# A recurrent-memory transformer and mixer kernel: each engine's instructions in one line of ranks, in place of a greedy pick

## The chip, the cores and the metric

One NeuronCore of one Trainium2 chip. The metric is the device time of one launch in microseconds (us), the median of the runs shown; lower is better.

## The reference, cut to what matters

```
x = A_x                                  # (1, 2048, 640), bf16
x = x + A(LN(x)); x = x + B(LN(x))       # layer 1
x = x + A(LN(x)); x = x + B(LN(x))       # layer 2, the same weights

A(x): mem = mem0                         # 8 rows
  for s in range(64):                    # segments of 32 rows
    h = concat([mem, x[32*s : 32*s+32]]) # 40 rows
    q, k, v = h @ Wq, h @ Wk, h @ Wv     # 32 heads of 192
    p = softmax(mask(q @ k.T / sqrt(192)))
    o = (p @ v) @ Wo                     # 40 rows x 640
    mem = o[:8]; out[s] = o[8:]

B(x): h = gelu(LN(x) @ w1)               # 640 x 640
      hs = (quarters of h, shifted by 1 or 2 rows down or up) @ w2
      x1 = x + hs
      return x1 + gelu(LN(x1) @ w3) @ w4 # 640 x 1536, 1536 x 640
```

The eight memory rows that come out of a segment go into the next one, so the 64 segments of a layer run one after the other.

## The kernel before

**Steps.** The kernel runs 69 steps, `t` = 0 to 68. Step `t` computes attention on segment `t` of layer 1 and on segment `t` - 5 of layer 2 (`LAG = 5`), as two "lanes" side by side in the same matmuls. Steps 0 to 4 have the first lane alone, steps 64 to 68 the second alone; the 59 steps between them have both. From step 2 on, every second step also starts a "chunk" of B (64 rows of each lane): `chunk` holds the layer norms, w1, w2 and w3, `chunk_end` w4 and the stores. So the kernel has a period of two steps, called a pair below: an even step, which carries `chunk`, and an odd one.

**Work of a step.** The 32 heads are taken in eight groups of four. The names below are those of the inner functions of `attention_step`:

| function | engine, lines | what it does for a group |
|---|---|---|
| `keys_queries.fn` | TensorE (PE), L1106 | keys (`psk`) and queries (`psq`), 6 or 18 matmuls at a time |
| `fk`, `fk2`, `fq` | VectorE (DVE) L1125 and L1132, ScalarE (ACT) L1117 | copies of keys and queries to SBUF |
| `values3.fv`, `values.fv` | PE, L1162 (two lanes), L1202 (one) | values of two groups; the array is split into 32 or 64 wide columns |
| `v_copy.fe` | ACT L1142 (with one lane DVE too) | copies of the values |
| `attend.fs` | PE, L1222 | scores `pss` |
| `f1`, `f2`, `f3` | DVE L1234, ACT L1241, DVE L1245 to L1247 | mask and row minimum, exponential, normalization |
| `f4`, `f5` | PE L1257, ACT L1265 | transposes of the probabilities, copy to `PT` |
| `f6`, `f7` | PE L1274, ACT L1282 | probabilities times values, copy to `oT` |
| `project.f8` | PE, L1300 | two blocks of 15 matmuls with Wo, accumulated over all groups in `psy` |

When all 16 blocks of `f8` are in, DVE copies the memory rows (`fm`, L1327) into the next step's `hT`, whose first keys and queries wait for that. In the chunk, `transposes` (L1380) follow a layer norm (L1354 to L1356 on DVE, L1364 on GpSimd, L1370 on DVE), and the sums of w2 (L1660) enter one through L1677.

**Weights.** A part of Wq, Wk, Wv and all of Wo is kept in SBUF (`res_tile`, L963); the rest is streamed in every step through a ring of 12 buffers `wst` (`load_pair`, L979), and w1 to w4 through 3 buffers `wstB` (`load_b`, L1015). All these loads are issued by SyncE (SP), one after the other.

**The order.** The functions above are not called where they stand. `Plan.add` records each as an operation with its engine, an estimated duration, a due time, its predecessors and the PSUM or ring buffers that it needs; `Plan.place` then decides in which order all 20,033 operations are issued, and with it which of the interchangeable buffers each gets. In `place`, time goes on by estimates. An operation is a candidate once its predecessors are placed. Of an engine's candidates that could start within 0.12 us (PE) or 0.05 us (the others) of the earliest, the one with the lowest rank `op.pr` goes first; while PE is in a split-array mode, operations of that mode go ahead. The two queues of loads, `wa` and `wb`, are each in order of due time. The flag `keep` holds back one or two PSUM buffers from some operations.

The rank is a number from the table `RANK` plus the start of the step. All even steps with two lanes share one list (`step0`), the odd ones another (`step1`); the one-lane steps have `step0a`, `step1a`, `step0b`, `step1b`; steps 0, 1 and 68 have lists of their own, and the chunks four kinds.

A load can also get a wait that the data does not ask for: where the plan holds it back (`op.paced`), it waits for a PE operation placed shortly before.

Of the kernel before, what the change touches and what calls it, by code (L numbers as in the profile page):

```python
# [20 lines left out]
LAG = 5  # L21
# [26 lines left out]
LAT = 0.07  # L48
# [21 lines left out]
        "apply_ln.f": (40.666, 77.653, 60.325, 136.543,),  # L70
        "chunk.f1": (149.945,),
        "chunk.f2": (216.417,),
        "chunk.f3": (155.176,),
        "chunk.fe": (75.977,),
        "chunk.fe3": (198.054,),
        "chunk.fel": (228.91,),
        "chunk.fhr": (61.777,),
        "chunk.fhs": (218.218,),
        "chunk.fk0": (191.856,),
        "chunk.fk1": (121.846,),  # L80
        "chunk.fs": (49.786, 151.703,),
        "chunk.ft": (158.562,),
        "chunk.fw": (42.803, 169.943, 29.392, 148.529, 90.1, 11.697, 135.335, 134.874, 211.529, 268.509, 163.859,
            -14.712, 124.067,),
        "chunk.fx": (133.776,),
        "chunk.fx0": (137.067, 177.953,),
        "chunk.fxu": (58.634,),
        "gelu.f1": (101.378, 21.338, 126.119, 33.51, 52.11, 75.508, 54.74,),
        "gelu.f2": (-97.492, 94.341, 84.288, 173.304, -56.927, 147.711, 109.223,),
        "gelu.f3": (153.483, 118.045, 87.113, 42.669, 49.105, 150.693, -76.347,),  # L90
        "gelu.f4": (215.512, 20.666, 98.392, 164.337, 98.395, -19.815, 38.198,),
        "ln_ops.f1": (134.07, 148.183,),
        "ln_ops.f2": (224.099, 88.099,),
        "load_b.fn": (223.389, -19.177, -20.646, 90.639, 9.322, 217.551, 18.597, 62.818, 70.516, 168.406, 246.054,
            -38.876, 264.694,),
        "transposes.f": (51.17, -12.814, 36.007,),
    },
    "chunk_0": {
        "apply_ln.f": (94.572, 40.674, 99.984, 157.869,),
        "chunk.f1": (191.077,),  # L100
        "chunk.f2": (131.998,),
        "chunk.f3": (54.83,),
        "chunk.fe": (62.439,),
        "chunk.fe3": (144.847,),
        "chunk.fel": (188.349,),
        "chunk.fhr": (111.798,),
        "chunk.fhs": (35.35,),
        "chunk.fk0": (279.891,),
        "chunk.fk1": (172.8,),
        "chunk.fs": (-35.996, 198.001,),  # L110
        "chunk.ft": (-130.725,),
        "chunk.fw": (65.065, 183.661, 25.703, 78.053, 99.658, 101.601, 99.809, 59.563, 88.798, 111.146, 143.476,
            55.339, -78.899,),
        "chunk.fx": (54.138,),
        "chunk.fx0": (87.873, 36.59,),
        "chunk.fxu": (99.398,),
        "gelu.f1": (126.71, -29.076, 155.641, 51.835, 147.033, 124.243, 168.393,),
        "gelu.f2": (78.921, 274.88, 137.606, 151.483, 27.132, 58.196, 59.089,),
        "gelu.f3": (117.084, 46.08, 158.262, 0.249, 28.271, 95.39, 62.133,),
        "gelu.f4": (76.679, 104.557, -54.1, 110.658, 151.139, 33.853, 164.863,),  # L120
        "ln_ops.f1": (54.318, 149.368,),
        "ln_ops.f2": (235.942, 114.803,),
        "load_b.fn": (92.037, 17.038, 113.343, 48.931, -19.849, 68.172, 137.659, 98.815, 95.648, 183.418, 66.865,
            -12.07, 10.81,),
        "transposes.f": (-24.285, -1.559, -116.16,),
    },
    "chunk_1": {
        "apply_ln.f": (60.831, 149.44, 32.185, 134.603,),
        "chunk.f1": (170.297,),
        "chunk.f2": (62.735,),  # L130
        "chunk.f3": (43.465,),
        "chunk.fe": (95.975,),
        "chunk.fe3": (173.951,),
        "chunk.fel": (25.923,),
        "chunk.fhr": (176.191,),
        "chunk.fhs": (114.575,),
        "chunk.fk0": (206.574,),
        "chunk.fk1": (238.724,),
        "chunk.fs": (118.505, 102.403,),
        "chunk.ft": (99.656,),  # L140
        "chunk.fw": (-11.005, 57.564, 28.334, 134.891, 126.429, 158.993, 107.2, 142.84, 61.226, 94.852, 116.376,
            8.48, 114.245,),
        "chunk.fx": (83.335,),
        "chunk.fx0": (-20.333, 52.005,),
        "chunk.fxu": (148.101,),
        "gelu.f1": (28.271, 94.572, 36.624, 95.274, 14.56, 53.144, 63.864,),
        "gelu.f2": (37.136, 133.251, 134.956, 64.362, -76.106, 19.116, 161.678,),
        "gelu.f3": (21.295, -102.923, 161.628, 76.35, 65.44, 109.028, 174.762,),
        "gelu.f4": (174.545, 97.124, 142.652, 141.694, 60.364, 76.871, 132.958,),
        "ln_ops.f1": (162.228, 148.321,),  # L150
        "ln_ops.f2": (235.566, 107.308,),
        "load_b.fn": (145.113, 225.966, 12.701, -9.013, 112.357, 1.949, 84.958, -9.104, -18.176, 31.005, 172.224,
            55.576, 114.018,),
        "transposes.f": (96.899, 66.044, -38.11,),
    },
    "chunk_2": {
        "apply_ln.f": (8.202, 39.685, 192.795, 133.254,),
        "chunk.fe": (190.072,),
        "chunk.fe3": (84.469,),
        "chunk.fel": (198.164,),  # L160
        "chunk.fhr": (103.491,),
        "chunk.fhs": (185.145,),
        "chunk.fk0": (111.508,),
        "chunk.fk1": (163.798,),
        "chunk.fs": (161.524, 76.874,),
        "chunk.ft": (26.979,),
        "chunk.fw": (98.577, 144.019, -18.584, 159.176, 43.005, 108.193, 111.764, 32.15, -26.496, 216.749, 7.779,
            10.758, 3.409,),
        "chunk.fx": (120.989,),
        "chunk.fxu": (78.836,),  # L170
        "chunk.fz": (166.304,),
        "gelu.f1": (62.309, 171.702, 48.166, -74.106, 94.517, 171.311, 114.397,),
        "gelu.f2": (67.833, 145.055, 4.726, 204.533, 99.365, 118.038, 58.3,),
        "gelu.f3": (23.209, 88.075, 155.923, 172.275, 169.817, 76.866, 110.477,),
        "gelu.f4": (248.488, 170.71, 206.421, 32.421, 181.585, 40.743, 63.89,),
        "ln_ops.f1": (58.912, 167.818,),
        "ln_ops.f2": (190.32, 246.267,),
        "load_b.fn": (216.599, 23.043, 172.357, 161.103, 73.744, 88.447, 84.661, -8.871, 26.089, 19.475, 66.634,
            -0.164, 128.784,),
        "transposes.f": (155.883, 38.197,),  # L180
    },
    "chunk_end": {
        "apply_ln.f": (74.666,),
        "chunk_end.fc": (70.51, -35.564, 44.026,),
        "chunk_end.fs": (87.765, 84.744,),
        "chunk_end.fst": (209.154, 130.81,),
        "chunk_end.ft4": (41.154,),
        "chunk_end.fw": (135.537, 72.945, 58.938, 109.724, 176.111, -20.18,),
        "chunk_loads.f": (216.414, 82.152, 214.202, 66.482, 114.965,),
        "ln_ops.f1": (147.277,),  # L190
        "ln_ops.f2": (123.156,),
        "load_b.fn": (12.735, -55.921, -67.147, 236.411, 24.651, 132.479,),
    },
    "chunk_end_0": {
        "apply_ln.f": (55.229,),
        "chunk_end.fc": (45.352, 234.489,),
        "chunk_end.fs": (50.063, 260.419,),
        "chunk_end.fst": (132.001,),
        "chunk_end.ft4": (146.259,),
        "chunk_end.fw": (318.093, 80.971, 109.238, 226.518, 174.396, 112.588,),  # L200
        "chunk_loads.f": (173.64, 236.626, 258.971,),
        "ln_ops.f1": (164.537,),
        "ln_ops.f2": (229.895,),
        "load_b.fn": (-80.145, 213.968, -54.408, 81.572, -5.558, 174.34,),
    },
    "chunk_end_1": {
        "apply_ln.f": (202.88,),
        "chunk_end.fc": (212.408, 176.723, 92.891,),
        "chunk_end.fs": (267.017, 127.574,),
        "chunk_end.fst": (80.687,),  # L210
        "chunk_end.ft4": (92.094,),
        "chunk_end.fw": (-44.134, 54.695, -10.468, 58.676, 84.616, 115.287,),
        "chunk_loads.f": (114.578, 103.494, 47.28, 166.009, 84.391,),
        "ln_ops.f1": (114.276,),
        "ln_ops.f2": (159.369,),
        "load_b.fn": (21.697, 78.816, -48.919, 11.318, 1.33, -117.781,),
    },
    "chunk_end_2": {
        "apply_ln.f": (134.851,),
        "chunk_end.fc": (113.219, 106.317, 211.498,),  # L220
        "chunk_end.fs": (59.427, 147.204,),
        "chunk_end.fst": (183.717, 30.774,),
        "chunk_end.ft4": (172.85,),
        "chunk_end.fw": (73.12, 14.739, 137.062, -11.873, 7.708, 235.266,),
# [351 lines left out]
class Plan:  # L576
# [57 lines left out]
    def place(self):  # L634
        in_queue = {}
        head = {}
        for q, lst in self.queues.items():
            lst.sort(key=lambda o: (o.due, o.i))
            for k, o in enumerate(lst):
                in_queue[o.i] = (q, k)  # L640
# [1293 lines left out]
```

## Time and profile before

| | |
|---|---|
| median of 3 runs | 3257.11 us (3255.47 to 3259.9) |
| profiled execution: span from first to last instruction | 3252.3 us |
| profiled execution: own time | not listed apart from the span; the span lies 4.8 us under the median |
| PE matmuls / weight loads (PEld) busy | 3142.1 us (97%) / 2780.2 us (85%) |
| DVE / ACT / POOL busy | 2274.2 us (70%) / 1833.8 us (56%) / 269.7 us (8%) |
| read from HBM | 816.98 MB, 253 GB/s over the span |
| granted TensorE clock | 0.992 of full speed on the mean |

Matmuls are pipelined: a matmul's row in the profile (200 ns for most) lasts longer than its share of the engine. Weight loads (99 ns, one ahead of each matmul) show how closely the stream is packed. An engine name with "<-" behind it tells what ended an idle time: the instruction that released it, or "issue", where the profile shows no release.

### The profile page before, as it was taken

The page shows a single profiled execution, that of the slowest core. Times are in us where ns is not written, and L with a number is a line of the kernel's source. Part 1 is how long each engine was busy: PE and PEld are TensorE (multiplying, and loading weights), DVE is VectorE, ACT ScalarE, POOL GpSimd, SP SyncE. Part 2 cuts the span into 40 slices and gives each one's busy share as a digit, 9 for nine tenths or more (in the row PEclk, how much of TensorE's full clock was granted, in tenths as well). Part 3 has the DMA queues.
Part 4 walks back from the last instruction along what each step waited for, and adds up shares of the span by engine and source line. Part 5 has one row for each costly group of instructions (what it writes and reads, how often), then busy time and mean ns, then how long its engine had stood idle before and what let it go on. Part 6 is the DMA issues. An engine that isn't in the chain of part 4 may idle for free.

```text
span 3252.3 us, 173204 instructions
## 1 busy us (share of the span) xinstructions
PE 3142.1 (97%) x77159; PEld 2780.2 (85%) x77161; DVE 2274.2 (70%) x7377; ACT 1833.8 (56%) x4217; POOL 269.7 (8%) x510
## 2 busy tenths in 40 slices
PE   5889999999999999999999999999999999999987
PEld 4778888888888888888888888888888888888776
DVE  3566777777777777777777777777777777767665
ACT  2335565666566656655566566556656665556443
POOL 0000000000000000000000000000000000000000
PEclk8999999999999999999999999999999999999999
DMA  9787777778777877787778777877877787778876
GB/s 365 271 274 252 241 264 259 243 242 266 258 243 242 279 243 240 246 271 253 242 248 273 238 242 257 270 237 248 269 251 244 243 271 251 241 246 274 276 269 209
DMA packets 409716, 833.46 MB, mean 256 GB/s; under 512 B 39650, under 2 KB 207279, under 8 KB 408968
## 3 DMA queue, kind: packets, MB, share of 16 engines
q1 hardware_dynamic: 401704, 809.47, 74.7%
q8 instruction: 604, 9.90, 1.2%
q0 software_dynamic: 7104, 12.84, 1.2%
q14 instruction: 144, 1.18, 0.1%
q10 hardware_dynamic: 160, 0.08, 0.0%
HBM read 816.98 MB, written 5.24 MB: 253 GB/s over the span
## 4 chain that ended last, share of the span: by engine, by line
PE 85%; ACT 8%; DMA 3%; issue 2%; DVE 2%; SPq 0%; POOL 0%; POOLq 0%; ACTq 0%; DVEq 0%
PE psk L1106 17%; PE psq L1106 17%; PE psv L1162 13%; PE psy L1300 13%; PE pss L1222 5%; PE pso L1274 4%; ACT V L1142 4%; PE psh L1723 4%; PE y L1769 3%; PE pst L1257 2%; PE psv L1202 2%; ACT oT L1282 1%; PE psh L1601 1%; PE hs L1660 1%; DMA wst<-in_A_Wq_dram 1%
## 5 line engine op out<-in xcount | busy, mean ns | idle before, releaser
L1106 PEld LDWEIGHTS <-wst 128*128 128x128 bf16 x19872 | 800.8, 99 | 50.3 <-issue 34.7
L1142 ACT CAST V<-psv 96x384 bf16<-96x384 f32 (+4 forms) x1264 | 589.5, 473 | 330.6 <-PE psv L1162 271.8
L1300 PE MATMUL psy<-oT,wo 128*128 128x80 bf16 (+1 forms) x16560 | 700.2, 200 | 21.6 <-DMA wo<-in_A_Wo_dram 8.9
L1300 PEld LDWEIGHTS <-wo 128*128 128x128 bf16 x16560 | 628.6, 99 | 43.2 <-issue 31.4
L1106 PE MATMUL psk<-hT,wst 128*128 128x80 bf16 (+1 forms) x9936 | 526.3, 200 | 15.1 <-DVE hT L1327 9.6
L1106 PE MATMUL psq<-hT,wst 128*128 128x80 bf16 (+1 forms) x9936 | 505.2, 200 | 4.7 <-DMA wst<-in_A_Wq_dram 3.6
L1117 ACT CAST qT<-psq 128x480 bf16<-128x480 f32 (+1 forms) x552 | 291.3, 528 | 380.3 <-PE psq L1106 301.1
L1162 PEld LDWEIGHTS <-hT 128*32 128x32 bf16 (+1 forms) x11840 | 295.1, 96 | 161.1 <-issue 8.9
L1132 DVE CAST kT<-psk 64x160 bf16<-64x160 f32 (+1 forms) x1104 | 339.3, 307 | 130.4 <-PE psk L1106 74.9
L1282 ACT CAST oT<-pso 128x480 bf16<-128x480 f32 (+1 forms) x552 | 292.3, 529 | 213.4 <-PE pso L1274 196.8
L1162 PE MATMUL psv<-wv,hT 128*32 128x384 bf16 (+1 forms) x5920 | 344.4, 328 | 0.7 <-issue 0.7
L1162 PE MATMUL psv<-wst,hT 128*32 128x384 bf16 (+1 forms) x5920 | 342.2, 326 | 0.0
L1245 DVE TENSOR_REDUCE sm<-Pm 80x4 f32<-80x320 bf16 (+2 forms) x552 | 249.8, 452 | 121.9 <-ACT Pm L1241 117.2
L1234 DVE CUSTOM_DVE_ANT_1 pss<-pss,mask 80x320 f32<-80x320 f32 (+2 forms) x552 | 258.5, 468 | 105.7 <-PE pss L1222 86.5
L1241 ACT ACTIVATE Pm<-pss,sm 80x320 bf16<-80x320 f32 (+2 forms) x552 | 279.2, 506 | 90.9 <-DVE kT L1132 50.0
L1106 PE MATMUL psq<-hT,wq 128*128 128x80 bf16 (+1 forms) x6624 | 321.0, 200 | 5.3 <-DMA wq<-in_A_Wq_dram 4.0
L1106 PE MATMUL psk<-hT,wk 128*128 128x80 bf16 (+1 forms) x6624 | 321.3, 200 | 5.0 <-issue 3.6
L1265 ACT COPY PT<-pst 80x320 bf16<-80x320 bf16 (+2 forms) x552 | 221.5, 401 | 167.6 <-PE pst L1257 161.8
L1125 DVE CAST kT<-psk 128x320 bf16<-128x320 f32 (+1 forms) x552 | 252.6, 458 | 39.5 <-PE pss L1222 24.4
L1247 DVE TENSOR_TENSOR Pm<-Pm,sm 80x320 bf16<-80x320 bf16 (+2 forms) x552 | 255.9, 464 | 33.7
L1106 PEld LDWEIGHTS <-wk 128*128 128x128 bf16 x6624 | 267.2, 99 | 6.8 <-issue 6.6
L1106 PEld LDWEIGHTS <-wq 128*128 128x128 bf16 x6624 | 265.9, 100 | 6.4 <-DMA wq<-in_A_Wq_dram 4.2
(131 smaller groups left out, 3732.7 us busy)
## 6 DMA issues: line engine op xcount, KB each, us to landing
wst<-in_A_Wk_dram SPq DMA_DIRECT2D x556, 384.0 KB, 4.5
wst<-in_A_Wq_dram SPq DMA_DIRECT2D x556, 384.0 KB, 4.7
wst<-in_A_Wv_dram SPq DMA_DIRECT2D x418, 384.0 KB, 4.7
wstB<-in_B_w_dram SPq DMA_DIRECT2D x495, 320.0 KB, 4.4
wstB<-in_B_w_dram SPq DMA_DIRECT2D x132, 160.0 KB, 4.1
wo<-in_A_Wo_dram SPq DMA_DIRECT2D x8, 960.0 KB, 12.3
wv<-in_A_Wv_dram SPq DMA_DIRECT2D x2, 1536.0 KB
xw<-in_A_x_dram POOLq DMA_DIRECT2D x32, 77.5 KB, 4.7
```

What stands on the lines that cost most here:

```text
L1106: nc.tensor.matmul(out=o[:, cc, 0:W], lhsT=wv(kc, GW * j + cc * P, GW * j + (cc + 1) * P), rhs=h[:, kc, cw:cw + W], start=begin(pq), stop= ...
L1117: nc.scalar.copy(out=qT[:, :, c0:c0 + N], in_=T(pq)[:, :, off:off + N])
L1125: nc.vector.tensor_copy(out=k4[:, :, 0::3, c0:c0 + N], in_=p4[:, :, 0::2, off:off + N])
L1132: copy(out=k4[r0:r1, :, jj, c0:c0 + N], in_=p4[r0:r1, :, 1, off:off + N])
L1142: (nc.vector.tensor_copy if e == "DVE" else nc.scalar.copy)(out=v_part(*dst), in_=a_)
L1162: nc.tensor.matmul(out=o[32 * u:32 * u + n3, :], lhsT=left[:, kc, 32 * g3:32 * g3 + n3], rhs=wv(kc, a, a + GWH), start=(kc == 0), stop=(kc ...
L1234: nc.vector.tensor_tensor_reduce(out=o, in0=o, in1=maskt.unsqueeze(1).to_broadcast([NR, HG, N]), scale=-scale, scalar=3.0e38, op0=ALU.add, ...
L1241: nc.scalar.activation(out=Pb[0:NR, :, 0:N], in_=o, func=ACT.Exp, bias=sm_[0:NR, 0:1], scale=-1.0)
L1245: nc.vector.tensor_reduce(out=sm_[0:NR, 2:2 + HG], in_=Pb[0:NR, :, 0:N], axis=AX.X, op=ALU.add)
L1247: nc.vector.tensor_tensor(out=Pb[0:NR, :, 0:N], in0=Pb[0:NR, :, 0:N], in1=sm_[0:NR, 6:6 + HG].unsqueeze(2).to_broadcast([NR, HG, N]), op=A ...
L1282: nc.scalar.copy(out=o_[:, :, off:off + N], in_=T(pso)[:, :, 0:N])
L1300: nc.tensor.matmul(out=o[:, m, cw:cw + W], lhsT=wo[:, cc, m * P:(m + 1) * P], rhs=o_[:, cc, 0:W], start=st, stop=True, skip_group_check=True)
```

## The change

`Plan.place` no longer chooses. Each engine's operations are sorted once by rank, and the engine takes them strictly in that order; an operation whose predecessors or buffers are not there yet holds up all that stand behind it. The two queues of loads become one line on SP, `keep` is no longer read, and no mode goes ahead of another. `RANK` holds new numbers, in units of 0.1 ns. The lists are also cut differently: `step0` and `step1` serve steps 7 to 61; steps 2 to 6 (`head2` to `head6`) and 62 to 67 (`tail0` to `tail5`) have a list each, and so have the first three and the last chunks. The operations, their instructions, predecessors and estimated durations stay as they are.

```
-        op.pr = due if k >= len(ranks) else self.base + ranks[k]
+        op.pr = round(10000 * due) if k >= len(ranks) else round(10000 * self.base) + ranks[k]
...
     def place(self):
-        in_queue = {}
-        head = {}
-        for q, lst in self.queues.items():
-            lst.sort(key=lambda o: (o.due, o.i))
...
         engines = sorted({o.e for o in self.ops})
-        cand = {e: [] for e in engines}
+        lines = {e: sorted((o for o in self.ops if o.e == e), key=lambda o: (o.pr, o.i)) for e in engines}
+        at = dict.fromkeys(engines, 0)
...
-            for c, (k, n) in need.items():
+            for c, n in need.items():
                 fs = self.free_slots[c]
-                if len(fs) < n + k:
+                if len(fs) < n:
                     return None
...
             for e in engines:
-                t = free[e]
-                lst = cand[e]
...
+                if at[e] == len(lines[e]):
                     continue
-                lim = m + (0.12 if e == "PE" else 0.05)
-                stay = e == "PE" and mode
-                s, o = min((so for so in vals if so[0] <= lim),
-                           key=lambda so: (so[1].mode != mode if stay else False, so[1].pr, so[1].i))
-                if best is None or s < best[0]:
+                o = lines[e][at[e]]
+                if o.n:
+                    continue
+                s = est(o, free[e])
+                if s is not None and (best is None or s < best[0]):
                     best = (s, o)
...
+    def step_tag(t):
+        if t < 2 or t == T_A - 1:
+            return "first" if t == 0 else "second" if t == 1 else "end"
+        if t <= LAG + 1:
+            return f"head{t}"
+        if t >= NSEG - 2:
+            return f"tail{t - NSEG + 2}"
+        return f"step{t % 2}"
...
     def kind(c):
-        if c < 2:
-            return "_0" if c == 0 else "_1"
-        return "" if 2 * c + 2 < NSEG else "_3" if 2 * c + 2 == T_A - 1 else "_2"
+        if c <= 2:
+            return f"_{c}"
+        return f"_tail{c - NSEG // 2 + 2}" if c >= NSEG // 2 - 2 else ""
```

Of `RANK`, the part that orders the projections and products at the end of the odd steps (before, then after):

```
-        "attention_step.project.f8": (70.337, -8.063, 71.936, 39.082, 155.009, 32.579, 165.885, 251.385, 109.215,
-            94.346, 143.76, 134.678, 65.876, 57.25, 145.21, 80.87,),
+        "attention_step.project.f8": (164161, 155084, 205823, 229807, 258570, 270785, 358397, 400141, 352513,
+            366635, 417766, 411882, 426788, 432672, 438556, 444440,),
```

For the end of an odd step this gives the following orders on PE, read from the two built programs (number behind #: the group for `fs`, `f4`, `f6`; the block for `f8`, two to a group; the pair's part for `fv`):

```
before: f6#5 f8#9 fs#7 f4#6 f8#8 fv#6 fv#7 f8#11 f6#6 f4#7 f8#10 f8#13 f6#7 f8#12 f8#15 f8#14
after:  f6#5 fs#7 f4#6 fv#6 fv#7 f8#7 f6#6 f4#7 f8#11 f8#10 f6#7 f8#12 f8#13 f8#14 f8#15
```

and for the end of an even one, up to its last projections:

```
before: fs#7 f4#6 f8#11 f8#8 f6#6 f8#10 f8#9 f8#13 f4#7 f8#12 f6#7 (3 products of w3 and f8#15, f8#14)
after:  f4#6 f8#7 f8#9 f6#6 f8#8 f8#10 f8#12 f4#7 f8#11 f8#13 f6#7 (3 products of w3 and f8#15, f8#14)
```

## The prediction

> **What bounds the kernel now.** I read the page first, then the busy times by stretch, then the waits of the weight loads, then the timeline at one place that repeats.
>
> The page says that matmuls fill the span except at its two ends.
>
> ```profile
> PE 3142.1 (97%) x77159; PEld 2780.2 (85%) x77161; DVE 2274.2 (70%) x7377; ACT 1833.8 (56%) x4217; POOL 269.7 (8%) x510
> ...
> PE   5889999999999999999999999999999999999987
> PEld 4778888888888888888888888888888888888776
> ```
>
> By stretches (each engine's busy us, instructions in brackets, then clock, DMA share, GB/s):
>
> ```profile
> 0.00:100.00 100.00, 59.23 (x1174) 48.25 (x1175) 29.36 (x107) 18.71 (x52) 7.53 (x23) 0.78 0.95 344
> 400.00:1500.00 1100.00, 1093.03 (x26750) 976.10 (x26738) 804.73 (x2571) 664.50 (x1486) 91.30 (x171) 1.00 0.77 254
> 1500.00:2800.00 1300.00, 1290.45 (x31524) 1150.77 (x31521) 947.42 (x3028) 781.45 (x1749) 113.09 (x210) 1.00 0.76 252
> 3000.00:3200.00 200.00, 181.06 (x4835) 154.60 (x4835) 126.07 (x450) 84.01 (x236) 17.91 (x34) 0.99 0.78 263
> ```
>
> The first 100 us are bound by DMA (0.95 busy). The steps with one lane leave PE idle (18.9 of 200 us). In the middle the matmul row is idle for 7.0 + 9.6 us of 2400. A pair takes 93.4 us there (starts of the memory copy L1327 of every second step), so that is 0.64 us a pair. Weight loads tell more, from 300 to 2850 us:
>
> ```profile
> PEld L1106 <- issue: 21.2, 56, 0.4
> PEld L1300 <- issue: 19.4, 82, 0.3
> PEld L1222 <- ACT V L1142: 17.5, 55, 0.3
> PEld L1222 <- issue: 9.1, 27, 0.3
> PEld L1257 <- issue: 8.9, 28, 0.3
> PEld L1723 <- issue: 8.6, 27, 0.3
> PEld L1162 <- issue: 8.4, 29, 0.9
> PEld L1257 <- DVE Pm L1247: 8.3, 26, 0.3
> PEld L1274 <- issue: 4.7, 27, 0.2
> ```
>
> The counts are multiples of 27, the number of pairs, so these gaps repeat in every pair: 106 us, 3.9 a pair. Eight gaps of 0.32 us a pair follow the eight value blocks and belong to the array's split; the change keeps these blocks. One of 0.43 opens each even step, behind the copy of the memory rows, and no order can fill it. About 0.95 us a pair is left (3.9 - 2.56 - 0.43) that an order may win or lose. The timeline shows the clearest:
>
> ```profile
> 1047.80 0.35 PEld L1274 LDWEIGHTS <-V 80*128 80x128 bf16 x8
> 1048.09 0.64 PEld L1300 LDWEIGHTS <-wo 128*128 128x128 bf16 x16
> 1048.32 0.56 ACT L1282 CAST oT<-pso 128x480 bf16<-128x480 f32 x1 [0.75 <-PE pso L1274]
> 1048.93 1.10 PEld L1300 LDWEIGHTS <-wo 128*128 128x128 bf16 x29 [0.21 <-issue]
> ```
>
> Group 7's product ends, one block of projections (15 loads) runs, then the next block's second load waits 0.21 us until the cast that it reads is done.
>
> The trace leaves open which of the two PE rows to count. [...]
>
> **The change in the middle.** Nothing is added or removed: 20,033 operations with the same predecessors before and after, and in a pair of the middle 252 PE operations and 16 changes of the array's split on both sides. Only covers change: how much PE work stands between an operation and the one that needs its result through ACT or DVE. The needs, from rows:
> - `f6` to its first `f8`: 0.84 us, from 1048.09 (PE moves on) to 1048.93 (cast done and seen).
> - `f4` to `f6`: 0.70 us. The copy L1265 takes 0.42, and 0.28 of the above 0.84 is not the cast (0.84 - 0.56).
> - `fs` to `f4`: 2.65 us. L1234 0.49 + 0.11, L1241 0.53, L1245 to L1247 0.48 + 0.18 + 0.49, and 0.37 for five hand-overs, an estimate from the 0.28 above.
>
> The covers, from the programs' orders, with 0.55 us for a block `f8` (half of 1.10 us for 29 loads), 0.22 for 6 key matmuls, 0.29 for `f6`, 0.15 for `f4`:
> - Before, odd step: groups 6 and 7 have 0.68 and 0.54 from `f6` to `f8`, so 0.16 + 0.30 short; groups 0 and 1 have 0.66 and 0.64 from `f4` to `f6`, 0.10 short. Even step: group 7 has 0.54 from `f4` to `f6`, 0.16 short (L1274's 0.2 above), and 0.80 to `f8`, 0.04 short. Sum 0.76 a pair.
> - After, odd step: groups 6 and 7 have 1.51 and 1.07 to `f8`, since two blocks stand where one stood; `f4` to `f6` is short only in group 1 (0.66). Even step: group 7 has 1.07 to `f6` and keeps 0.80 to `f8`. Sum 0.08.
> - `fs` to `f4` is nowhere short: least cover 2.87 before, 2.79 after.
>
> That is 0.68 us a pair less. A second gain: before, one value block (L1162, 8.4 us of gaps in the view) follows w4's products, whose 320 columns keep the loads waiting 0.26 us; after, all follow shorter matmuls. I take half, 0.15.
>
> Against it stand queues. ACT and DVE run their instructions in the program's order, before as after, but that order is new. At the odd step's end group 6's cast stands behind group 7's copy L1265 and the last value copies (four of 0.47 us), and with it its need of 0.84 comes to 1.5 or 1.7, against 1.51: 0 to 0.2 us. In the even step the cover between w2's last product and `transposes` (L1380) falls from 6.1 to 5.0 us. Before, the chain between took 4.4 us (L1660 ends at 983.2, L1370 at 987.55), so 0.6 is left. I take 0.15 for both; the bounds are 0 and 0.55.
>
> Middle: -0.68 - 0.15 + 0.15 = -0.68 us a pair, over 28 pairs (29.5 two-lane pairs, the first and last with lists of their own): -19 us. By the bounds of the queues and of the 0.26: -0.3 to -0.95 a pair, -8 to -27 us.
>
> **Loads.** SP's order is new in every step; a load that waits for its buffer holds up all behind it, as it did before. A load takes 4.5 us from issue to landing (median, wst). Between what frees a load and the first matmul that reads it, the tightest in a pair has 5.6 us of PE work before and 5.5 after; under 6 us stand 8 a pair before and 6 after. I cost it at nothing: that spare 1 us hides it, and in the middle waits for `wst` now add up to 1.1 us. Step 0 needs 31.6 MB before its last Wo block, the same bytes in another order; 0.95 of DMA time leaves nothing to win. That the first keys now wait for 9 MB in place of 2 costs nothing, since step 0 has 31 us of PE work in 91.
>
> **The ends.** By the same three needs (for one lane 2.02, 0.57 and 0.64 us, the same rows at its shapes) the covers of steps 1 to 4 are short by 11.7 us in all before and 7.1 after, those of steps 64 to 68 by 10.7 and 5.3: 10 us less. Against that the ends have 18 more changes of the array's split (586 in all for 568). A value block costs 0.32 us on leaving and about 0.1 on entering, so a change 0.2: +4. Net -6; bounds 0 and -10, since DMA is 0.76 to 0.87 busy there and may take over waits.
>
> **Sum.** -19 - 6 = -25 us. On the profiled execution: 3252.3 to 3227 us; on the median, 4.8 us above that span: 3257 to 3232 us.
>
> **Rivals.**
> - *All of the order's gaps go*: 0.95 + 0.15 a pair and 10 us at the ends, -41 us, 3216. For it: gaps below the view's resolution shrink too. Against: the queues above.
> [...]
> - *Slower: DVE's line lags.* DVE is 0.73 busy in the middle. `transposes` of the second layer norm waits on seven DVE instructions and one on GpSimd; if something ahead of them holds the line, PE has 0.6 us to spare, and all of attention queues behind that wait. From a lag of 1.5 us on the kernel is slower (0.6 to spare, then 0.68 of the pair and 6/28 of the ends eaten); at 2 us it costs 1.4 - 0.7 = +0.7 a pair, +20 us less 6 at the ends: 3271. Against: in the trace that chain has only one attention operation (L1245 to L1247) in it. [...]
> - *Nothing changes*: excluded, the built orders differ on every engine.
>
> **Numbers.** My forecast has 0.70, all gaps 0.13, matmul idle alone 0.10, DVE's lag 0.07. About 0.2% (6.5 us) is what a measurement of this kernel can tell from no change. The forecast's own bounds are -8 - 0 = -8 and -27 - 10 = -37, so 3220 to 3249. The range 3213 to 3250 takes in these and most of the two rivals beside them; slower is left out. Faster by over 0.2% (under 3250.6): the first two and part of the third, 0.86; within: 0.07; slower: 0.07.
>
> **What would show it.** In the profile after, from 300 to 2850 us: the gaps of L1274 (4.7 us) and L1162 (8.4) mostly gone, those of L1300 (19.4) near 9, L1106 unchanged; a pair of 92.7 us by the starts of L1327; steps 64 to 67 shorter by some 4 us. New gaps at L1380 or waits for `wst` would make me wrong, and a pair of 93.4 us or more would refute the sum of covers.

## The result and the profile after

| | before | after |
|---|---|---|
| median, same chip | 3256.29 us (4 runs, 3252.24 to 3259.9) | 3235.56 us (4 runs, 3234.03 to 3238.1) |
| ratio | | 0.9933, 95% interval 0.9918 to 0.9948 |
| profiled execution | span 3252.3 us | 3234.03 us, span 3232.2 us |
| pair in the middle (median) | 93.42 us | 92.79 us |
| steps 7 to 61 | 2526.2 us | 2508.4 us |

Forecast: 3232 us. The same program, run on two more occasions, gave 3232.37 us (ratio 0.9918, 0.9898 to 0.9938) and 3231.84 us (0.9905, 0.9886 to 0.9924). After the change every line number of the kernel's body is larger, by 290 in attention: L1106 became L1396, L1162 L1452, L1222 L1512, L1257 L1547, L1274 L1564, L1282 L1572, L1300 L1590, L1327 L1617; L1380 became L1670. All stretches of steps here run between starts of the memory copy (L1327 and L1617; in one-lane steps L1332 and L1622), as in the prediction's pair. "Steps 7 to 61" runs from the copy of step 7 to that of step 61, which is 27 pairs; the other stretches hold the whole of the steps that they name.

The 2508.4 us are the lowest of the six profiled executions that have the changed kernel's middle (three of the changed kernel, three from experiment 3): 2508.4 to 2513.2, mean 2510.6, so 13.0 to 17.8 us less than the one profiled execution before, 15.6 on the mean. The median steps repeat far better: in all six an odd step takes 43.88 to 43.90 us (44.13 before) and an even one 48.90 (49.28 before). That is 0.63 us a pair, 17.0 over 27 pairs.

The page of the changed kernel, busy times and the slices:

```profile
PE 3123.3 (97%) x77161; PEld 2775.7 (86%) x77161; DVE 2262.7 (70%) x7377; ACT 1836.5 (57%) x4217; POOL 270.6 (8%) x510
...
PE   4889999999999999999999999999999999999997
PEld 3778888888888888888888888898898888888776
```

By stretches (columns as in the prediction):

```profile
0.00:100.00 100.00, 52.06 (x1245) 44.58 (x1246) 30.83 (x115) 19.34 (x56) 7.54 (x23) 0.90 0.97 353
400.00:1500.00 1100.00, 1095.54 (x26909) 982.87 (x26906) 805.23 (x2587) 669.40 (x1493) 92.50 (x172) 1.00 0.78 256
1500.00:2800.00 1300.00, 1293.64 (x31781) 1159.91 (x31778) 948.26 (x3050) 789.62 (x1762) 113.91 (x210) 1.00 0.78 254
3000.00:3200.00 200.00, 180.74 (x4897) 153.94 (x4893) 127.58 (x460) 81.52 (x236) 14.22 (x27) 1.00 0.84 280
```

More weight loads fit into the same time (26,906 for 26,738 from 400 to 1500 us), and the idle of the matmul row shrinks by only 2.5 of 1100 us. The gain lies in the weight loads' waits, 300 to 2850 us:

```profile
PEld L1396 <- issue: 47.0, 139, 0.4
PEld L1590 <- issue: 9.1, 29, 0.3
PEld L1512 <- issue: 8.6, 27, 0.3
PEld L1670 <- issue: 8.3, 26, 0.3
PEld L1547 <- issue: 8.3, 26, 0.3
PEld L1512 <- ACT qT L1407: 4.5, 25, 0.2
PEld L1396 <- DMA wst<-in_A_Wk_dram: 1.4, 4, 0.6
```

Sums of the whole view: 107 us before, 90 after, so 17 us, as much as the 27 median pairs lost. Gone are the product's wait (L1274, 4.7), the one ahead of a value block (L1162, 8.4) and, of the projections' 19.4, all but one gap of 0.3 us a pair (9.1), which stands behind a value block. One place of each of the first two, before the change:

```profile
1003.07 0.31 PEld L1274 LDWEIGHTS <-V 96*128 96x128 bf16 x7 [0.17 <-issue]
...
1034.00 1.42 PEld L1162 LDWEIGHTS <-hT 128*32 128x32 bf16 x40 [0.26 <-issue]
```

L1396 did not stay at 21.2 us: the eight gaps of 0.32 us behind the value blocks are still eight a pair, but more of them now fall on keys and queries and fewer on scores (L1222 had 17.5 + 9.1). The 8.3 us at L1670 are such a gap too, one in each pair, as the chunk's L1723 had before (8.6), and not a wait of `transposes` for the layer norm. New is 0.2 us in every pair on the queries' copy.

The timeline shows the cover at work: the cast L1572 of one group runs beside two blocks of projections (30 loads in one piece), that of the next beside the first two of four (60 loads), and no load waits.

```profile
1043.85 1.14 PEld L1590 LDWEIGHTS <-wo 128*128 128x128 bf16 x30
...
1044.47 0.56 ACT L1572 CAST oT<-pso 128x480 bf16<-128x480 f32 x1
...
1044.93 0.35 PEld L1564 LDWEIGHTS <-V 80*128 80x128 bf16 x8
...
1045.22 2.22 PEld L1590 LDWEIGHTS <-wo 128*128 128x128 bf16 x60
...
1045.45 0.56 ACT L1572 CAST oT<-pso 128x480 bf16<-128x480 f32 x1 [0.25 <-PE pso L1564]
```

### The profile page after: what moved, and what is told of

It is laid out like the page before. It is cut to its first block, busy times and chain, and to the rows that moved or that the text cites. A ratio compares the mean times of both kernels' runs of the same rounds, so it can differ in the third digit from the quotient of the medians.

```text
span 3232.2 us, 173085 instructions
## 1 busy us (share of the span) xinstructions
PE 3123.3 (97%) x77161; PEld 2775.7 (86%) x77161; DVE 2262.7 (70%) x7377; ACT 1836.5 (57%) x4217; POOL 270.6 (8%) x510
## 4 chain that ended last, share of the span: by engine, by line
PE 91%; DMA 3%; ACT 3%; issue 1%; DVE 1%; SPq 0%; POOL 0%; ACTq 0%; POOLq 0%; DVEq 0%
PE psy L1590 17%; PE psk L1396 17%; PE psq L1396 16%; PE psv L1452 16%; PE pss L1512 5%; PE pso L1564 4%; PE y L2058 3%; PE psh L2012 3%; PE pst L1547 3%; PE psv L1492 2%; ACT V L1432 2%; PE psh L1890 1%; DMA wst<-in_A_Wk_dram 1%; PE hs L1949 1%; PE psv L1670 1%
## 5 line engine op out<-in xcount | busy, mean ns | idle before, releaser
L1396 PEld LDWEIGHTS <-wst 128*128 128x128 bf16 x19872 | 815.5, 99 | 62.2 <-issue 31.1
L1432 ACT CAST V<-psv 64x384 bf16<-64x384 f32 (+5 forms) x1264 | 589.8, 476 | 240.9 <-PE psv L1452 187.7
L1590 PE MATMUL psy<-oT,wo 128*128 128x80 bf16 (+1 forms) x16560 | 693.2, 200 | 8.3 <-issue 3.9
L1590 PEld LDWEIGHTS <-wo 128*128 128x128 bf16 x16560 | 624.9, 99 | 25.4 <-issue 20.0
L1396 PE MATMUL psk<-hT,wst 128*128 128x80 bf16 (+1 forms) x9936 | 554.8, 200 | 17.8 <-DMA wst<-in_A_Wk_dram 14.4
L1396 PE MATMUL psq<-hT,wst 128*128 128x80 bf16 (+1 forms) x9936 | 545.6, 200 | 4.1 <-issue 2.5
L1407 ACT CAST qT<-psq 128x480 bf16<-128x480 f32 (+1 forms) x552 | 291.5, 528 | 388.6 <-PE psq L1396 366.0
L1452 PEld LDWEIGHTS <-hT 128*32 128x32 bf16 (+1 forms) x11840 | 294.9, 96 | 153.8 <-issue 0.3
L1572 ACT CAST oT<-pso 128x480 bf16<-128x480 f32 (+1 forms) x552 | 293.2, 531 | 184.8 <-PE pso L1564 183.6
L1452 PE MATMUL psv<-wv,hT 128*32 128x384 bf16 (+1 forms) x5920 | 343.8, 328 | 0.0
L1452 PE MATMUL psv<-wst,hT 128*32 128x384 bf16 (+1 forms) x5920 | 341.4, 326 | 0.0
L1396 PE MATMUL psk<-hT,wk 128*128 128x80 bf16 (+1 forms) x6624 | 320.7, 200 | 15.3 <-DVE hT L1617 9.3
L1396 PE MATMUL psq<-hT,wq 128*128 128x80 bf16 (+1 forms) x6624 | 320.3, 200 | 9.9 <-DMA wq<-in_A_Wq_dram 7.5
L1555 ACT COPY PT<-pst 80x320 bf16<-80x320 bf16 (+2 forms) x552 | 221.0, 400 | 170.4 <-PE pst L1547 164.1
L1396 PEld LDWEIGHTS <-wk 128*128 128x128 bf16 x6624 | 270.7, 99 | 32.7 <-issue 29.3
L1396 PEld LDWEIGHTS <-wq 128*128 128x128 bf16 x6624 | 266.3, 99 | 21.9 <-issue 14.0
```

Of the source, the lines that this page charges most:

```text
L1396: nc.tensor.matmul(out=o[:, cc, 0:W], lhsT=wv(kc, GW * j + cc * P, GW * j + (cc + 1) * P), rhs=h[:, kc, cw:cw + W], start=begin(pq), stop= ...
L1407: nc.scalar.copy(out=qT[:, :, c0:c0 + N], in_=T(pq)[:, :, off:off + N])
L1432: (nc.vector.tensor_copy if e == "DVE" else nc.scalar.copy)(out=v_part(*dst), in_=a_)
L1452: nc.tensor.matmul(out=o[32 * u:32 * u + n3, :], lhsT=left[:, kc, 32 * g3:32 * g3 + n3], rhs=wv(kc, a, a + GWH), start=(kc == 0), stop=(kc ...
L1572: nc.scalar.copy(out=o_[:, :, off:off + N], in_=T(pso)[:, :, 0:N])
L1590: nc.tensor.matmul(out=o[:, m, cw:cw + W], lhsT=wo[:, cc, m * P:(m + 1) * P], rhs=o_[:, cc, 0:W], start=st, stop=True, skip_group_check=True)
```

## Experiments

**1. Undo the covers, one at a time.** Theory: the order between a product and its projections makes the gain. Rival: something else in the new order does. In the odd step three ranks change: block 11 goes back ahead of group 6's product and block 13 ahead of group 7's, as before the change. In the even step one rank changes: block 11 goes ahead of group 7's transposes, so that one block in place of two is left behind them.

```
 "step1": "attention_step.project.f8":       # odd_end
-  ..., 352513, 366635, 417766, 411882, 426788, 432672, 438556, 444440
+  ..., 352513, 366635, 412000, 404000, 426788, 418000, 438556, 444440
 "step0": "attention_step.project.f8":       # even_end; both_ends has both
-  ..., 410960, 423013, 416278, ...
+  ..., 410960, 420000, 416278, ...
```

> The changed kernel with four ranks of step1's projections put back, so that the end of every odd step in the middle has the order of before on PE (one block of projections between group 6's copy of probabilities and its product, one between group 7's product and the block that reads its cast); nothing else moves. Theory of covers, ACT's order left out: group 6 is 0.16 us short and group 7 0.30, so a pair grows by 0.46 us, from 92.79 to 93.25. Theory of covers with ACT's new order counted (the copy to PT of group 7 now stands ahead of group 6's cast, so group 6's block waits 0.21 + 0.42 + 0.56 + 0.07 = 1.26 us after f4 against 0.55 of cover): group 6 is 0.7 short and group 7 0.3, a pair grows by 1.0 us, to 93.8. Rival, the order at step ends is hidden anyway and the gain came from elsewhere (the value blocks' neighbours, the queues): within 0.1 us of 92.79.

> The changed kernel with one rank of step0's projections put back: at the end of every even step in the middle one block of projections instead of two stands between group 7's transposes and its product. Theory of covers: 0.16 us short (the gap in the trace of before was 0.17 to 0.23), a pair grows from 92.79 to 92.95 or 93.0 us, and the gap returns at the product's weight loads. Rival, hidden anyway: 92.79.

> Both of these together. Theory of covers: the two add up, since the ends lie 44 us apart: with ACT's order counted a pair of 93.95 us, 27.5 pairs x 1.16 = +32 us on the changed kernel, about 3267 us, slower than the kernel before; without ACT's order 93.4 us, +17 us, 3253 us, level with the kernel before. Rival, hidden anyway: 3236 us.

Measured: the median odd step went from 43.89 us to 44.71, the median even one from 48.90 to 49.08, in each edit alone and in both together. So the pair grows by 0.83 (odd), 0.18 (even) and 1.01 us (both), and the two add up. Times: 3251.8 and 3234.88 us (one run each), and with both 3258.21 us (10 runs), 0.9994 of the kernel before (0.9981 to 1.0006). In the middle two short edits thus more than undo the change's 0.63 us a pair: steps 7 to 61 take 2535.9 us, 9.7 more than in the kernel before, and the time as a whole is level with it only because the rest of the kernel is shorter. The rival of a hidden order is out. Of the two theories the one with ScalarE's order counted is nearer (1.0 for the odd step, 1.16 for both), but it gave too much, in the time as well (3267 us). What no run put back is the 0.31 us a pair ahead of the value block; that is read from the two views alone.

The waits of the weight loads with both edits (line numbers are 2 lower here: L1588 is the projection L1590), and one place in the timeline (L1553 is the copy L1555, L1570 the cast L1572):

```profile
PEld L1394 <- issue: 46.0, 135, 0.4
PEld L1588 <- issue: 31.0, 84, 0.6
```

```profile
1048.95 0.42 ACT L1553 COPY PT<-pst 80x320 bf16<-80x320 bf16 x1 [0.44 <-PE pst L1545]
1049.27 0.56 ACT L1570 CAST oT<-pso 128x480 bf16<-128x480 f32 x1
...
1049.88 0.56 PEld L1588 LDWEIGHTS <-wo 128*128 128x128 bf16 x14 [0.58 <-issue]
...
1051.52 1.10 PEld L1588 LDWEIGHTS <-wo 128*128 128x128 bf16 x29 [0.21 <-issue]
```

The projections' waits rise from 9.1 to 31.0 us, 0.81 a pair, and the two places add up to 0.79 us: the odd step's loss, in the very gaps that the covers name. It is more than the 0.46 that lack of cover alone gives, because group 6's cast (1049.27) stands behind group 7's copy to `PT` (1048.95) on ScalarE in the new order, and that copy waits for group 7's transposes. The even step's 0.18 does not show in this view as a wait; there group 7's product takes 0.47 us from its first load to the next operation's, for 0.29 in the changed kernel (both in step 20; first the even edit, whose line numbers are 1 lower, then the changed kernel):

```profile
1088.81 0.54 PEld L1563 LDWEIGHTS <-V 96*128 96x128 bf16 x8
1089.28 0.86 PEld L2011 LDWEIGHTS <-wstB 128*128 128x128 bf16 x15
```

```profile
1094.07 0.35 PEld L1564 LDWEIGHTS <-V 96*128 96x128 bf16 x8
1094.36 0.86 PEld L2012 LDWEIGHTS <-wstB 128*128 128x128 bf16 x15
```

**2. The new wait on the queries.** Group 6's scores of the odd step are moved behind other work.

```
 "step1": "attention_step.attend.fs":
-  (47638, 93196, 121166, 160968, 217199, 267592, 341448, 375977,)
+  (47638, 93196, 121166, 160968, 217199, 267592, 345000, 375977,)
```

> The changed kernel with one rank moved: in odd steps of the middle the scores of group 6 stand behind group 5's transposes instead of ahead of them. In the profile of the changed kernel these scores wait about 0.25 us in every pair for the copies of their queries. Theory of covers: 0.15 us of PE work goes into the wait, a pair shrinks from 92.79 to 92.65 us, the whole by 3 to 4 us. Rival: the wait moves to the next product of the chain (the softmax starts no earlier than before) and a pair stays at 92.79.

> The kernel with group 6's scores of the odd steps later, again, on the same chip as the changed kernel. Theory, each program meets pauses and half-clock stretches at its own places: near 3224 us, 8 to 12 us below the changed kernel. Rival, the occasion's doing: within 3 us of the changed kernel.

> The changed kernel itself, nothing edited, beside the kernel with group 6's scores of the odd steps later, which ran at 3223.95 us and 0.988 of the kernel before, against 3235.56 and 0.9933 for the changed kernel on another occasion. In the traces the two differ by under 0.1 us per pair in the middle and by 8 us in the one-lane steps, whose order is identical. Theory, the one-lane steps lose time to pauses and half-clock stretches that each program meets at its own places: the changed kernel again shows steps 1 to 4 near 167 us with three half-clock windows, and about 3235 us; the difference of some 8 to 12 us to the other kernel is repeated. Rival, the difference is the chip's or the occasion's: both kernels within 3 us of each other here, and steps 1 to 4 within 2 us.

Measured: 3223.95 us (0.988, 0.9861 to 0.9899) on one chip; on another 3226.07 (0.9894, 0.9878 to 0.9911) beside 3232.37 (0.9918, 0.9898 to 0.9938) for the changed kernel. The four runs of each there do not overlap (3224.14 to 3226.37, 3229.07 to 3239.7), so this version is the fastest of all. The wait on L1407 is gone from the view and the median odd step is 0.15 us shorter (43.74 for 43.89), as the theory of covers had it, which is 4 us over 28 odd steps; steps 7 to 61 show 1.7 us of it (mean 2508.9 us of two executions, 2510.6 of six with the changed kernel's middle), which is less than those six differ among themselves. The rest of the 6 us stays open: side by side the difference was neither the 8 to 12 us of the theory nor under the rival's 3. The theory that each program has fixed places for its pauses fell: the changed kernel, run again, had steps 1 to 4 at 163.4 us, not 167, and two stretches at half clock there, not three.

**3. Middle and ends apart.** The lists of steps 0 to 6 and 64 to 68, and of the chunks beside them, get numbers that reproduce the order of the kernel before on every engine; the middle stays the changed kernel's.

```
 "head3": ...                                # and likewise every list of both ends
-  "attention_step.attend.f6": (54650, 125152, 256338, 289647, 348185, 378677, 432280, 445702,),
+  "attention_step.attend.f6": (253713, 266122, 323388, 364337, 398770, 440248, 506083, 515949,),
```

> Steps 0 to 6 and 64 to 68 with the chunks beside them in the order of the kernel before, on every engine; everything between in the changed kernel's order. The prediction's sum gives the middle -19 and the ends -6: steps 7 to 61 stay at 2508 us, and the rest goes back from 718.6 us to the 721.8 of the kernel before, with steps 64 to 67 from 167.5 to about 171: 3239 to 3242 us. Rival, in the one-lane steps pauses and half-clock windows set the time and not the covers of the order: the rest lies anywhere between 710 and 722 us, as it does among kernels whose ends have one and the same order (710.3 to 718.6), and steps 64 to 67 between 165 and 169.

> Steps 0 to 6 and the chunks beside them in the order of the kernel before, on every engine; all else in the changed kernel's order. With both ends in the old order the time was 3239.33 us, 7 above the changed kernel beside it. The prediction gave covers of -4.6 us to steps 1 to 4 and -5.4 to steps 64 to 68, and +4 to the changes of the split, so by it the head alone costs about 2 to 3 us: 3234 to 3236. Rival, from the trace with both ends old: steps 64 to 67 were no longer there (166.4 us against 168.3), while step 0 (90.5 against 88.6), steps 1 to 4 (165.3 against 163.4) and steps 5 to 7 (143.1 against 140.3) all were; then the head alone costs 5 to 7 us, 3237 to 3240, and step 0 shows a stretch of some 20 us at half clock near 55 us, which the changed order doesn't have.

> Steps 64 to 68 and the chunks beside them in the order of the kernel before; all else in the changed kernel's order. By the prediction 2 to 4 us slower than the changed kernel, and steps 64 to 67 longer by some 4 us than its 167.5 to 168.3. Rival, the tail's order is worth nothing in steps 64 to 67 (165 to 169 us, as with both ends old) and about 2 us after step 67 (62.3 us against 60.3): 0 to 3 us slower.

> The changed kernel itself, so that the kernels with one end in the old order have it beside them on the same chip: 3229 to 3236 us; steps 64 to 67 at 166 to 169 us, steps 1 to 4 at 162 to 167.

Measured, first chip: before 3258.53 us, middle changed alone 3239.33 (3236.37 to 3244.01), all changed 3232.37. So the middle brings 19.2 us and the ends 7.0, though one of the four runs with all changed (3239.7) lies among those with the middle alone. Second chip: with the old head alone 3236.09 us (3230.8 to 3244.23), with the old tail alone 3236.34 (3231.41 to 3238.69), beside 3231.84 (3226.3 to 3236.24) for the changed kernel: 4.2 and 4.5, though the runs overlap and neither alone is certain.

A part of the 7.0 us belongs to neither order. Step 7, the first with the common list, takes 44.13 us in the kernel before and 43.84 to 44.07 in the changed kernel and the version of experiment 2, but 46.29 and 46.27 in the two runs with the old head. There the old order of the head meets the new order of the middle, and TensorE waits for a chain that in neither kernel holds it up (with the old head alone):

```profile
381.47 0.20 PEld L2112 LDWEIGHTS <-h2u 128*128 128x128 bf16 x5 [1.08 <-DVE h2u L1660]
...
382.56 1.12 PEld L1396 LDWEIGHTS <-wst 128*128 128x128 bf16 x30 [0.68 <-DVE kT L1415]
```

So some 2.2 of the 7.0 us, and of the 4.2 of the old head, are the price of the join, and about 4.8 are left for the ends.

One execution is too few to read the ends from. Means over the profiled executions, by order of the end (in brackets the lowest and highest; the runs of experiments 4 and 5 are left out; "after step 67" ends with the last VectorE instruction):

| stretch | old order (3) | new order (9) | difference |
|---|---|---|---|
| step 0 | 90.7 (90.5-90.8) | 89.0 (88.2-89.6) | -1.7 |
| steps 1-4 | 163.7 (161.8-165.3) | 163.4 (160.3-166.9) | -0.3 |
| steps 62-63 | 93.8 (93.2-94.3) | 92.9 (92.6-93.4) | -0.9 |
| steps 64-67 | 168.4 (166.4-170.8) | 166.0 (163.1-168.9) | -2.4 |
| after step 67 | 61.9 (61.5-62.3) | 60.3 (59.8-60.9) | -1.6 |

Step 0 and the time after step 67 are told apart without overlap. Up to the end of the span, with the output's transfers, the latter is 66.3 us (65.7 to 66.8) against 65.0 (64.0 to 65.9), which does overlap. In the one-lane steps the spread within one order is larger than the difference. For steps 64 to 67 the rival's 165 to 169 us was met with the old tail (168.1), and the prediction's 4 us more was met too against the changed kernel beside it (164.1): that stretch decides nothing in single executions. In step 0 the old order shows a stretch at half clock to its very end, which the new order doesn't have (75 to 90 us of the kernel before, then of the changed kernel):

```profile
75.00:90.00 15.00, 8.67 (x167) 7.95 (x168) 0.00 (x0) 1.07 (x3) 0.00 (x0) 0.50 1.03 350
```

```profile
75.00:90.00 15.00, 11.42 (x279) 10.21 (x277) 6.79 (x24) 5.54 (x16) 1.65 (x3) 0.84 0.90 305
```

In the old order TensorE has only 167 matmuls in these 15 us, all at clock 0.50, and DMA is full; the new order has 279 and is more than half at full clock. All three executions with the old head show it. That this is what the 1.7 us are is argued, not shown by a run of its own.

**4. What makes the one-lane steps vary.** The changed kernel's weight loads pause in the middle of runs of identical matmuls. First an execution with a pause, then the same six loads in another execution of the same program:

```profile
184.22 0.17 PEld L1396 LDWEIGHTS <-wst 128*128 128x128 bf16 x4
186.67 0.11 PEld L1396 LDWEIGHTS <-wst 128*128 128x128 bf16 x2 [2.28 <-issue]
```

```profile
183.59 0.23 PEld L1396 LDWEIGHTS <-wst 128*128 128x128 bf16 x6
```

Four loads, 2.28 us of nothing, two more; the other time all six in one piece. The pauses come at one place of TensorE's instruction stream. In the expectations they are counted by the rows of the weight-load engine from the program's start: 100 to 105 modulo 128 in steps 1 to 4, 6 to 13 in steps 64 to 67. In the changed kernel these rows hold 352 instructions of the sequencer (semaphores, nearly all) besides the loads, and that is why the number drifts. Counted by instructions (loads, matmuls and those of the sequencer) it does not: in steps 1 to 4 and 64 to 67 of all 14 profiled executions here, the kernel before among them, 122 of the 123 waits over 0.7 us that have no releaser stand at 193 to 195 modulo 256. The page counts the packets that carry instructions:

```profile
q8 instruction: 604, 9.90, 1.2%
```

604 packets of 16,384 bytes, and (2 x 77,161 + 352) / 256 = 604.2. The packet ahead of the pause above started at 184.28 and took 0.90 us; the loads go on 1.5 us after it ended. Theory: TensorE waits for its next block of instructions. Rival: the waits belong to the operations. Experiment: 48 more matmuls in step 0, ahead of group 7's scores, which overwrite their products.

```
-for n_, (i, w_, c, j) in enumerate(seq):
+for n_, (i, w_, c, j) in enumerate(([(0, 1, 0, 0)] * 48 if t == 0 and p_ == NG - 1 else []) + seq,
+                                   0 if t or p_ < NG - 1 else -48):
```

> The changed kernel with 48 more matmuls, each with its weight load, ahead of the scores of group 7 in step 0; their products are overwritten by the scores themselves, and all else is the same. In the changed kernel the mid-run pauses of steps 1 to 4 sit at weight loads whose number is 100 to 105 modulo 128, counted from the program's start, and in steps 64 to 67 at 6 to 13. Theory, they wait for the next block of 256 instructions of TensorE: the count with the 48 stays at 100 to 105 and 6 to 13, so that the pauses fall on matmuls 48 loads earlier than before, and operations that held one now run through. Rival, the pauses belong to the operations (a wait, a transfer, a buffer): they stay with the same matmuls, and the count goes to 20 to 25 (mod 128) in steps 1 to 4. The time itself: 0 to 2 us longer for the 48 matmuls in step 0 by either, and by the theory up to 8 us either way for where the half-clock windows then come.

Measured, 3230.34 us (one run): the pauses over 0.7 us without a releaser stay at 100, 101 and 104 (head) and 6, 6, 7 and 14 (tail, the last behind step 67), all at instruction 193 or 194 modulo 256, on other operations than before:

```profile
103.85 0.12 PEld L1396 LDWEIGHTS <-wq 128*128 128x128 bf16 x2 [1.72 <-issue]
...
154.32 0.10 PEld L1590 LDWEIGHTS <-wo 128*128 128x128 bf16 x1 [1.00 <-issue]
...
223.55 0.14 PEld L1590 LDWEIGHTS <-wo 128*128 128x128 bf16 x3 [0.93 <-issue]
```

Real waits of the order behave the other way, and so tell the two kinds apart: the ones of 0.60 and 0.68 us in the head (rows 11 and 30 of that count) repeat to 0.01 us in all three profiled executions of the changed kernel, and moved with their operations to 59 and 78, by exactly 48.

**5. Longer matmuls.** `ONE = 56` becomes `ONE = 80`: 24 more columns, never read, in the key, query and Wo matmuls of the one-lane steps.

> The changed kernel with 80 columns in place of 56 in the key, query and Wo matmuls of the one-lane steps (720 a step; what the 24 more columns hold is never read). A run of 128 such matmuls takes 4.6 us in place of 3.3, by 36 and 26 ns a matmul in the trace. Theory, the pauses that sit at one weight-load number modulo 128 wait for the next 16 KB of instructions, which take longer to come than 3.3 us but not longer than 4.6: those pauses (5 to 7 over 0.6 us in steps 1 to 4 of the changed kernel, 5 to 7 in steps 64 to 67) go to 0 or 1 each, and steps 1 to 4 get longer by less than the matmuls' 28.8 us, by 15 to 22. Rival, the pauses have a fixed cost whatever the matmuls' length: as many as before, and steps 1 to 4 longer by 27 to 30 us.

Measured: 3268.6 us (one run). At the fixed count one pause over 0.6 us is left in steps 1 to 4 and none in steps 64 to 67, as the theory has it. Steps 1 to 4 took 177.6 us, 13 more than the 164.7 of the changed kernel beside them: less than the theory's 15 to 22, and half of the 28.8 us of matmul work added. The other 16 us of that work are made up for elsewhere: the pauses at the count fell from 8.1 to 1.1 us, and the 6.8 us at half clock, worth some 3.4, are gone. The 5 to 6 us that are left stay open.

## Why the prediction was right, and where not

**What to count.** Here the weight loads, not the idle of the matmul row: the loads' waits fell by 17 us, the matmul idle by 2.5 + 3.2 us in 2400, and steps 7 to 61 by 17.8 (15.6 on the mean of six executions).

**Middle, -19: 17.0 by the median pairs, 13.0 to 17.8 by single profiled executions, 19.2 by the times of experiment 3, with the price of the join in it.** The mechanism is the one forecast, as experiment 1 shows. The terms, per pair: `f6` to `f8` and `f4` to `f6` were to give 0.68 and gave 0.38 (L1300) and 0.17 (L1274). The value block behind w4 was taken at 0.15, half of its 0.26; its gap of 0.31 (8.4 us) went whole. The queues' 0.15 were lost, but not where the text put them: neither group 6's cast nor `transposes` waits; the scores wait on the queries' copy for 0.17 (4.5 us over 27 pairs). So two terms were off by 0.13 and 0.16 and cancelled, and a third had the right size at another place: that the sum came so close (0.69 by these terms, 0.63 by the pairs) was in part luck. The bound of -0.3 a pair was too good by its own terms: with nothing from the value block and 0.55 for the queues it is -0.13, -4 us.

**Loads, nothing.** Right within a microsecond: waits for `wst` go from 0.8 to 1.7 us in 2550.

**Step 0, nothing.** Wrong by 1.7 us. The step of the working that failed is "0.95 of DMA time leaves nothing to win": the bytes were the same, but with the old order TensorE ran the last 15 us of the step at half clock throughout (167 matmuls), with the new one mostly at full clock (279). That this makes the 1.7 us is argued.

**Ends, -6.** The sum was about right (-4.8 by times without the join, -6.9 by the sum of the table), its content was not. The covers of the one-lane steps were to bring 10 us and the split changes to cost 4. What is told apart is 1.7 us in step 0 and 1.6 from step 67 to the last VectorE instruction; steps 1 to 4 gained nothing that can be told, and steps 64 to 67 some 2 of the 4 us. The step that failed is the use of the middle's covers there: between ten executions with one order in steps 1 to 4, the time goes with the pauses and the clock (last section). The first profiled pair shows only -2.3 us outside steps 7 to 61, since that execution of the changed kernel had the longest steps 1 to 4 of the nine.

**Rivals.** *All gaps go* is out by the time (3235.56 us for 3216) and by the new 4.5 us; the 9.1 us left at the projections stand behind a value block, and that rival never counted them. *DVE's line lags* did not decide, but was close: in the pair below `transposes` issue 0.27 us after the chain's last instruction ended, not 0.6, and between 300 and 2850 us they do wait for it once in the changed kernel (0.5 us) and five times in one execution of experiment 2's version (1.6 us).

```profile
985.10 0.55 POOL L1654 TENSOR_TENSOR st<-st,neghalf 128x1 f32<-128x1 f32 x1 [8.69 <-DVE st L1646]
...
986.08 0.43 DVE L1660 TENSOR_SCALAR vbg<-h2u,st 128x640 bf16<-128x640 bf16 x1
...
986.78 0.30 PEld L1670 LDWEIGHTS <-vbg 128*128 128x128 bf16 x5
```

## What to carry to other kernels

For each operation of the bottleneck engine that needs its own result back through another engine, write down the need (duration plus hand-over) and the cover (work placed between); the differences are what an order can win, and here two blocks in place of one at the end of the odd steps were worth 0.8 us of a 93 us pair, nearly half of it because of the new order of the copies on ScalarE. Then look where the other engines' lines put the copies in between, since the next wait appears there. Where the profile of one execution shows a difference of a few us at the ends, repeat the same program before explaining it.

## What was unexpected in the hardware

**Pauses at one count of instructions show where matmuls are short.** With 56 columns, 128 loads and matmuls take 3.3 us (26 ns each), and pauses of up to 2.28 us (ahead of 186.67 us, above) appear at one place of every 256 instructions; with 80 columns (4.6 us, 36 ns each) they all but vanish, in the one-lane steps of experiment 5 (one over 0.6 us is left) as in the middle, whose matmuls have 80 columns in every version: between steps 5 and 63 an execution has none to four of over 0.5 us at that place. Busy DMA engines are not needed for it: a pause of 1.3 us stands at 119.87 us, in a stretch with a DMA share of 0.05:

```profile
118.00:129.00 11.00, 8.81 (x194) 6.52 (x191) 4.27 (x17) 3.23 (x10) 0.00 (x0) 0.84 0.05 17
```

By the page's 604 packets of 16,384 bytes for 154,674 instructions a packet carries 256. That TensorE waits for the next packet at these places is the author's theory: experiments 4 and 5 fit it, and no row of a trace shows it.

**Half clock comes behind pauses.** In this row the clock is 0.84, as one stretch of 3.4 us at 0.5 makes it. Over ten executions with the same order in steps 1 to 4 (that with 48 more matmuls among them), a least-squares fit gives 156.3 us + 0.58 x (sum of pauses over 0.5 us at instruction 193 to 195) + 0.52 x (us at half clock). It leaves 0.6 us of a spread of 2.5: pauses of 3.7 to 9.1 us and 0 to 11 us of half clock go with 157.6 to 166.9 us. Three numbers fitted to ten points show that they go together, and not yet that one makes the other. The trace shows the length and the rate: in steps 1 to 4 of the changed kernel three stretches of 3.41 us at 0.50, from 120.71, 165.09 and 188.98 us on. The pauses ahead of them, of 1.3, 1.7 and 2.3 us, end at 119.87, 163.40 and 186.67 us. Not every pause brings it: none follows that of 1.93 us ahead of 3093.74 us in the same execution, whose clock is 1.00 from 192.4 to 3180 us. What decides stays open.
